# Output projection and memory update in fp16 and column strips, and nine query projections of branch B done in halves in slots 0 to 8

## The chip, the cores and the metric

One core of a Trainium2 chip. The metric is the device time of one execution in microseconds (us). The engines are named as in the profile: PE (TensorE matmul), PEld (TensorE weight load), DVE (VectorE), ACT (ScalarE), POOL (GpSimd), SP (SyncE, which issues most DMAs).

## The reference, cut

```python
# x [1, 2048, 512]; 32 heads of 16; A: 4 segments of 512; B: plain attention
g  = sigmoid((x * gate_w).sum(-1, keepdims=True))
# A: per segment s, M [16 x 16] and z [16] per head carried along
logits = qs @ ks^T * 16**-0.5 + causal_mask(512)
a_dot  = softmax(logits) @ vs
phi    = lambda t: where(t > 0, t + 1, exp(t))
a_mem  = (phi(qs) @ M) / (phi(qs) @ z + 1e-6)
o_s    = sigmoid(beta) * a_mem + (1 - sigmoid(beta)) * a_dot
M += phi(ks)^T @ vs;  z += phi(ks).sum(over positions)
a = concat(o_s) @ A_wo
# B: q, k, v = split(x @ B_wqkv)
b = (softmax(q @ k^T * 16**-0.5) @ v) @ B_wo
return g * a + (1 - g) * b
```

## The kernel before

**Numbers.** Inputs and weights are float32. A projection of x is made from two fp16 parts of each operand: `split` scales a tensor by a power of two and writes `hi` and `lo = raw - hi`. `TERMS = ((0,0),(0,1),(1,0))` are the three products kept, so one projection of a 512-token chunk for 128 channels is 12 matmuls of 512 columns (three terms, four blocks of 128 input channels). The scale comes from the largest magnitude: `peak` reduces on DVE (L379), `top` transposes the statistic on PE (L396) and reduces it, `spread` sends the factors to all partitions by small PE products (L407).

**Phase 1 (0 to 317.87 us).** Sixteen blocks, (group g of 8 heads, segment c) each. A block projects A's q and k (`qk_job`: `qk_mm` on PE, `qk_out` on ACT and DVE, and stores to DRAM by SP), runs A's memory chain, and does as many jobs of the list `fill` as `CUM` says. The memory chain of a block: `mem_out` (phi(q) times M), `mem_put` (transposes, L465, store), `mem_tr` (transposes of phi(k)), `mem_upd` (L488: phi(k) as weights, v with a column of ones as data, 136 columns, float32 in two passes, four 128-token blocks summed; the blocks on the diagonal are picked by a mask and added to M). `fill` holds 16 v projections of B and 24 q and k projections of B (g = 1 to 3); 36 of the 40 are done in the blocks, the last four in slot 0. Between jobs, `spill` puts in products that find the row maxima of the scores of the first units (L565 with the mask products L569; L587).

**Slots.** A unit is four heads against one 512-query chunk, of A (causal) or B (2048 keys). Slot k, of 32, has 37 steps n: 32 of B's unit 32+k and five of A's unit k. Each step (`t_group`) makes two score tiles, keys on partitions (L650, two heads in the two 64-row halves of PE, into a bank of the rotation `T3` = tb0, tb1, mb), then ACT takes the exponential (L656, `raw`), and POOL masks A's diagonal (L659). `pvs(k, n)` multiplies an earlier step's exponentials by v with a column of ones (`pv`, L672: four heads as four strips of 32 output rows in the bank pvb, float32 in two passes). Between the score products the plan puts `s_b` (L587) and DVE's reduction (L589) for the row maxima of the next unit. After n = 20 `m_chain` makes the negative maxima, `m_rows` (L620, n = 24) transposes them. At the end of a unit `fin_copy` (L678) copies pvb, and `fin_load`, `fin_rec`, `fin_bc`, `fin_norm` normalize in later steps.

**The order of the work** is written out: `extras(k)` gives what is done ahead of `pvs` at step n (`pre`) and behind it (`post`), `beside(k, it)` what is done with every second step (it = n // 2). Each engine works through its own list in this order. Four fill jobs stand in slot 0 at n = 0, 2, 4, 6.

**Output projection.** From slot 9 on, row tiles of 128 tokens of finished chunks: `out_split` (ACT copy, POOL subtract) makes `oh`, `ol` in fp32r; `out_mm` makes 12 matmuls for each branch a in two pieces of six (`PIECES`, at n = 1 and 12, `OUT_AT`) into a bank of the rotation (L743), ACT copies the piece (L747, L750) and POOL adds it to `yo` (L751). The two output weights are loaded and split in slots 1 to 4 (`load_wo`, `split_wo`). The last four row tiles are the tail behind slot 31 (`tail_mm`, L773).

Of the kernel before, what the change touches and what calls it, by code (L numbers as in the profile page):

```python
# [42 lines left out]
def gated_mix_kernel(ctx, tc, xt, wq, wk, wv, wo, beta, wqkv, wob, gate_w, out):  # L43
# [298 lines left out]
    def qk_mm(ws, w, c):  # L342
        b = misc()
        n = 0
        for xi, wi in TERMS:
            for k in range(4):
                nc.tensor.matmul(b, WS[ws][w][wi][:, k, :], (XH, XL)[xi][c][:, k, :], start=n == 0, stop=n == 11)  # L347
# [135 lines left out]
    def mem_upd(g, c):  # L483
        pk = PHI.pop((g, "k", c))
        vm = PHI.pop((g, "v", c))
        b = misc()[:, :8 * (E + 1)]
        for i in range(4):
            nc.tensor.matmul(b, pk[:, i, :], vm[:, i].rearrange("p h e -> p (h e)"),  # L488
                             start=i == 0, stop=i == 3)
# [726 lines left out]
```

## Time and profile before

| what | us |
|---|---|
| median of 3 runs (lowest, highest) | 1787.65 (1787.43, 1788.04) |
| the profiled execution | 1788.6 |
| its span in the profile | 1786.9 |
| phase 1 | 0 to 317.87 |
| slot 0 | 64.39 |
| slot 5 | 43.13 |
| slot 15 | 44.85 |
| tail | 1760.07 to 1786.9 |
| mean granted TensorE clock | 0.996 |

In the timeline's rows the columns are start, duration (us), engine, line of the kernel, operation, output<-inputs (partitions x elements and type), and the count of instructions merged into the row; in brackets the idle time ahead of it on its engine and what ended it. A duration of PE includes the pipeline, so that the pace of products is read from the starts of rows. In the rows by group the last numbers are busy time in all, mean ns of one, and the idle time ahead. `<-issue` is a wait that the profile ties to nothing.

### The profile page before, as it was taken

How to read it: one execution, taken by the hardware profiler on the slowest of the kernel's cores; microseconds unless marked ns; L12 is line 12 of the kernel's file. 1: busy time of each engine (PE TensorE's matmuls, PEld its weight loads, DVE VectorE, ACT ScalarE, POOL GpSimd, SP SyncE). 2: the span in 40 equal slices, each digit the busy share in tenths (PEclk: the TensorE clock that was granted, in tenths of full speed). 3: DMA queues.
4: the chain of work that ended last, by engine and by line, in shares of the span. 5: the costliest groups of instructions: out<-in, count | busy, mean ns of one | idle time of the engine just before them, and what ended most of it. 6: DMA issues, size and time to landing. Idle time of an engine off the chain costs nothing.

```text
span 1786.9 us, 43232 instructions
## 1 busy us (share of the span) xinstructions
PE 1756.5 (98%) x17269; PEld 613.8 (34%) x17269; DVE 1559.8 (87%) x1707; ACT 1476.2 (83%) x2797; POOL 363.1 (20%) x739
## 2 busy tenths in 40 slices
PE   8999999899999999999999999999999999999998
PEld 6554445222222222333233333333333333333325
DVE  7745786699999999999999999999999999999932
ACT  4444444599999999999999999999999999999993
POOL 5200000002222111222222222222222222222222
PEclk9999999999999999999999999999999999999999
DMA  5554534332323323232323232323222322323101
GB/s 200 160 151 149 152 108 116 76 80 77 96 80 101 82 64 82 64 94 64 94 64 94 64 93 65 90 68 85 72 79 79 83 75 79 79 78 80 47 29 63
DMA packets 156558, 158.85 MB, mean 89 GB/s; under 512 B 33628, under 2 KB 120636, under 8 KB 156356
## 3 DMA queue, kind: packets, MB, share of 16 engines
q1 hardware_dynamic: 153124, 149.29, 29.9%
q0 software_dynamic: 2944, 6.27, 1.4%
q8 instruction: 136, 2.23, 0.5%
q14 instruction: 66, 0.54, 0.1%
q10 hardware_dynamic: 288, 0.52, 0.1%
HBM read 103.39 MB, written 50.86 MB: 86 GB/s over the span
## 4 chain that ended last, share of the span: by engine, by line
PE 89%; DVE 8%; ACT 1%; DMA 1%; issue 1%; ACTq 0%; SPq 0%; DVEq 0%; POOLq 0%
PE pvb L672 34%; PE tb L650 13%; PE sbk L587 11%; PE mb L650 7%; DVE mxb L589 7%; PE tb L347 3%; PE tb L743 3%; PE sbk L565 2%; PE mb L347 2%; PE pvb L347 2%; PE sbk L317 2%; PE tb L317 2%; PE mb L743 1%; PE sbk L347 1%; PE pvb L317 1%; PE sbk L569 1%
## 5 line engine op out<-in xcount | busy, mean ns | idle before, releaser
L589 DVE TENSOR_REDUCE mxb<-sbk 128x2 f32<-128x1024 f32 x1024 | 1176.6, 1213 | 42.1 <-PE tb L650 19.3
L656 ACT ACTIVATE raw<-tb 128x512 f32<-128x512 f32 x1553 | 880.9, 599 | 49.2 <-PE tb L650 18.2
L672 PE MATMUL pvb<-raw,vb 128*17 128x256 f32 (+1 forms) x7824 | 636.9, 395 | 0.0
L587 PE MATMUL sbk<-kb,qb 64*128 64x512 f16 x2048 | 588.1, 380 | 5.8 <-DVE mxb L589 5.6
L656 ACT ACTIVATE raw<-mb 128x512 f32<-128x512 f32 x783 | 469.1, 599 | 23.7 <-PE mb L650 10.1
L650 PE MATMUL tb<-qb,kb 64*128 64x512 f16 x1339 | 461.7, 381 | 5.0 <-ACT raw L656 3.9
L650 PEld LDWEIGHTS <-kb 64*128 64x128 f16 x2048 | 122.9, 94 | 433.5 <-issue 414.8
L672 PEld LDWEIGHTS pvb<-raw,vb 128*17 128x17 f32 x7824 | 132.4, 95 | 397.0 <-issue 390.9
L650 PE MATMUL mb<-qb,kb 64*128 64x512 f16 x681 | 259.5, 381 | 0.7 <-ACT yp L750 0.7
L659 POOL TENSOR_SCALAR_AFFINE_SELECT raw<-raw 128x256 f32<-128x256 f32 (+1 forms) x320 | 115.3, 361 | 285.8 <-ACT raw L656 277.7
L573 DVE TENSOR_REDUCE mx<-sbk 128x2 f32<-128x1024 f32 (+1 forms) x128 | 133.8, 1087 | 6.7 <-PE sbk L569 5.6
L587 PEld LDWEIGHTS <-qb 64*128 64x128 f16 x2048 | 115.9, 94 | 26.9 <-issue 21.0
L672 PE MATMUL pvb<-raw,va 128*17 128x256 f32 (+2 forms) x1280 | 103.4, 383 | 3.7 <-ACT pvs L678 0.9
L701 POOL TENSOR_TENSOR rec<-rec,grow 128x16 f32<-128x16 f32 x30 | 6.6, 221 | 355.4 <-DVE rec L693 355.4
L713 POOL TENSOR_TENSOR o<-o,d 128x512 f32<-128x512 f32 x31 | 39.5, 1275 | 170.3 <-DMA d<-rd 168.2
L575 DVE TENSOR_REDUCE mx<-sbk 128x4 f32<-128x512 f32 x64 | 60.6, 947 | 12.6 <-PE sbk L569 12.6
L565 PE MATMUL sbk<-ka,qa 64*128 64x512 f16 (+3 forms) x512 | 70.6, 296 | 0.0
L751 POOL TENSOR_TENSOR yo<-yo,yp 128x512 f32<-128x512 f32 x36 | 45.8, 1272 | 80.7 <-ACT yp L750 76.8
L650 PE MATMUL tb<-qa,ka 64*128 64x512 f16 (+3 forms) x340 | 62.0, 302 | 0.0
L362 DVE SCALAR_TENSOR_TENSOR phi<-phe,phi 128x512 f32<-128x512 f32 x24 | 16.6, 692 | 51.2 <-ACT phe L361 51.2
L347 PEld LDWEIGHTS <-ws 128*128 128x128 f16 x384 | 37.9, 100 | 45.4 <-issue 6.1
L569 PE MATMUL sbk<-cmask,crows 64*128 64x64 bf16 x1024 | 52.6, 189 | 0.0
(343 smaller groups left out, 1507.1 us busy)
## 6 DMA issues: line engine op xcount, KB each, us to landing
vb<-vdB SPq DMA_DIRECT2D x16, 1088.0 KB
pd<-pvs SPq DMA_DIRECT2D x64, 256.0 KB
kb<-dB SPq DMA_DIRECT2D x60, 256.0 KB
dB<-st SPq DMA_DIRECT2D x64, 128.0 KB
dA<-st SPq DMA_DIRECT2D x64, 128.0 KB
o<-pd SPq DMA_DIRECT2D x64, 128.0 KB
d<-rd SPq DMA_DIRECT2D x63, 128.0 KB
kb<-dB SPq DMA_DIRECT2D x60, 128.0 KB
```

The costliest lines, as they stand in the source:

```text
L317: nc.tensor.matmul(b, x[:, n % 4, tl * 128:(tl + 1) * 128], (WVA if kd == "A" else WV)[wi][:, n % 4, :], start=n == 0, stop=n == 11)
L347: nc.tensor.matmul(b, WS[ws][w][wi][:, k, :], (XH, XL)[xi][c][:, k, :], start=n == 0, stop=n == 11)
L565: nc.tensor.matmul(b[:, j, c0:c0 + n], q_of(u)[r, p, i * 128:(i + 1) * 128], k_of(u, p)[r, :n], start=True, stop=False)
L569: nc.tensor.matmul(b[:, j, c0 + n - 128 + w.start:c0 + n - 128 + w.stop], crows[r, n2 - 1], cmask[r, n2 - 1, w], start=False, stop=n2 == 2)
L573: nc.vector.tensor_reduce(m[:, :, p, i], b[:, :, :n], axis=AX.X, op=OP.max)
L587: nc.tensor.matmul(b[:, j], q_of(u)[r, p, i * 128:(i + 1) * 128], k_of(u, p)[r, kc * C:(kc + 1) * C], start=True, stop=True)
L589: nc.vector.tensor_reduce(MXB[u][:, :, p, i, kc], b, axis=AX.X, op=OP.max)
L650: nc.tensor.matmul(bs[j][:, c0:c0 + w], k_of(u, h // 2)[r, 128 * it:128 * it + 128], q_of(u)[r, h // 2, q0:], start=True, stop=True)
L656: nc.scalar.activation(pt, bs[j], AF.Exp, scale=AT["esc", kd, qd // 2])
L659: nc.gpsimd.affine_select(out=m, in_=m, pattern=[[1, 128]] if n < 2 else [[0, 2], [1, 128]], compare_op=OP.is_ge, fill=0.0, base=0, channe ...
L672: nc.tensor.matmul(PVB[32 * h:32 * h + E + 1, q0 + lo:q0 + hi], vt[:, it, 4 * q + h, :], pt[:, lo:hi], start=it == 0 and lo == 0, stop=it ...
L743: nc.tensor.matmul(b, (AT["oh"], AT["ol"])[oi][:, g, a], (AT["wh"], AT["wl"])[wi][:, g, a], start=n == 0, stop=n == hi - lo - 1)
```

## The change

Two groups of edits.

*fp16 and strips.* The output weights and the normalized outputs become fp16 pairs: the largest magnitude of the two weights is found in phase 1 (`load_or` loads both in block 0 through POOL's queue into the third and second K buffers, `o_abs` in blocks 2 and 3, `top` in block 4, `o_rng` in block 5), the outputs are scaled by `so` (from the largest magnitudes of v and x; A's v statistic comes from a reduction of `WVA[0]` ahead of block 0), and `back_o` is put into the scale of ACT's copies. `out_mm` writes each product as four strips of 32 output rows; `PIECES` are (0,6), (6,9), (9,12), at n = 1, 12, 20. `mem_upd` makes four strips of 32 rows, each with the two heads that it keeps (34 columns), where all eight heads' columns were made. `m_rows` transposes fp16 operands (`ident16`) and m_chain drops a cast. The weights' load and split go to slots 5 and 6, and 6 and 7 (it = 2 and 12), with one multiply more for each half. The tail uses fp16.

*Halves.* `fill` has 31 jobs, all in the blocks; the nine q projections of B for g = 1 to 3 and c = 1 to 3 (`LATER`) are done one in each of slots 0 to 8. `q_piece` does one half: 12 matmuls of 256 columns into a bank of the rotation, two ACT copies (fp16 `st`, float32 `qraw`), one POOL subtract; behind the second half SP stores both parts. `Q_AT` puts the halves at n = 11 and 19 in slot 0 and n = 1 and 12 in slots 1 to 8. For this x's parts of chunks 1 to 3 and the weights of these jobs (`WQ`) stay in one tile `BIG` beyond phase 1; it later holds the fp16 output weights (`WHL`) and the tail's operands.

```diff
-OUT_AT = (1, 12)
-PIECES = ((0, 6), (6, 12))
+OLOAD = (0, 2, 3, 4, 5)
+Q_AT = ((11, 19), (1, 12))
+OUT_AT = (1, 12, 20)
+PIECES = ((0, 6), (6, 9), (9, 12))
+    def q_piece(g, c, x):
+        h = slice(256 * x, 256 * x + 256)
+        b = misc()[:, :256]
+        for n, (xi, wi, k) in enumerate([(xi, wi, k) for xi, wi in TERMS for k in range(4)]):
+            nc.tensor.matmul(b, WQ[g][wi][:, k, :], (XH, XL)[xi][c][:, k, h], start=n == 0, stop=n == 11)
+        if not x:
+            AT["qs"] = AT["L"].tile([128, 2, C], HF, name="qs")
+        st = AT["qs"]
+        raw = AT["L"].tile([128, 256], FT, name="qraw")
+        nc.scalar.activation(st[:, 0, h], b, AF.Copy, scale=xr[:, c:c + 1])
+        nc.scalar.activation(raw, b, AF.Copy, scale=xr[:, c:c + 1])
+        nc.gpsimd.tensor_tensor(st[:, 1, h], raw, st[:, 0, h], op=OP.subtract)
+        if x:
+            img = QKD["B", 0, g][:, :, c * C:(c + 1) * C]
+            for a in range(2):
+                nc.sync.dma_start(img[:, E * (1 - a):E * (1 - a) + E], st[:, a])
...
 def mem_upd(g, c):
-        b = misc()[:, :8 * (E + 1)]
+        b = misc()[:, :2 * (E + 1)]
         for i in range(4):
-            nc.tensor.matmul(b, pk[:, i, :], vm[:, i].rearrange("p h e -> p (h e)"),
-                             start=i == 0, stop=i == 3)
+            for j in range(4):
+                r = slice(32 * j, 32 * j + 32)
+                nc.tensor.matmul(b[r], pk[:, i, r], vm[:, i, 2 * j:2 * j + 2].rearrange("p h e -> p (h e)"),
+                                 start=i == 0, stop=i == 3)
...
 def m_rows(k):
-            nc.tensor.matmul(b[32 * a:32 * a + 32], m8[:, a], ident, start=True, stop=True)
+            nc.tensor.matmul(b[32 * a:32 * a + 32], m8[:, a], ident16, start=True, stop=True)
...
 def split_wo(g):
+            nc.gpsimd.tensor_scalar(raw, raw, ou, None, op0=OP.mult)
             nc.gpsimd.tensor_copy(AT["wh"][:, g, a], raw)
+    def load_or():
+        for a, w in enumerate((wo, wob)):
+            nc.gpsimd.dma_start(KBF[1 + a], w.rearrange("(k p) c -> p k c", p=128))
+    def o_abs(a):
+        peak(stat(("O", 0), 2)[:, a:a + 1], KBF[1 + a])
+    def o_rng():
+        spread(("O", 0), [(o2[:, 0], o2[:, 1])])
...
 def out_mm(c, t, a, x):
-            nc.tensor.matmul(b, (AT["oh"], AT["ol"])[oi][:, g, a], (AT["wh"], AT["wl"])[wi][:, g, a],
-                             start=n == 0, stop=n == hi - lo - 1)
+            for j in range(4):
+                r = slice(32 * j, 32 * j + 32)
+                nc.tensor.matmul(b[r], (AT["oh"], AT["ol"])[oi][:, g, a, r], (AT["wh"], AT["wl"])[wi][:, g, a],
+                                 start=n == 0, stop=n == hi - lo - 1)
-        nc.scalar.activation(y, b, AF.Copy)
+        nc.scalar.activation(y, b, AF.Copy, scale=back_o)
...
+        if n == 0:
+            peak(stat(("A", 0), 4)[:, 3:4], WVA[0])
...
-    CUM = (2, 4, 6, 9, 11, 13, 16, 18, 20, 22, 24, 27, 29, 32, 34, 36)
+    CUM = (2, 4, 6, 8, 10, 12, 14, 16, 18, 20, 22, 24, 26, 28, 30, 31)
+    LATER = [(g, c) for c in range(1, NC4) for g in range(1, 4)]
...
-        if not k:
-            for n in range(4):
-                pre[2 * n] = [fill[n - 4]]
+        if k < len(LATER):
+            for x, at in enumerate(Q_AT[k > 0]):
+                pre[at] = [todo(q_piece, *LATER[k], x)]
```

How the instructions stand on PE, at three places. First the beginning of slot 0. In the program before (L650 score products, tb and mb banks; L587 row-maximum products, sbk banks; L347 a projection of B's fill list, xp and xq the two parts of x):

```order
L465 MATMUL tb_139<-ident,om 128x128 x4
L650 LDWEIGHTS kb_89
L650 MATMUL tb_138<-qb_70,kb_89 128x512
L587 LDWEIGHTS qb_68
L587 MATMUL sbk_142<-kb_90,qb_68 128x512
...
L650 MATMUL mb<-qb_70,kb_89 128x512
L347 LDWEIGHTS wv_105
L347 MATMUL tb_139<-xp_99,wv_105 128x512
...
L347 MATMUL tb_139<-xq_103,wv_105 128x512
```

The changed program at the same place (L514 is L465 of before, L699 L650, L639 L587, L721 L672):

```order
L514 MATMUL pvb<-ident,om 128x128 x4
L699 LDWEIGHTS kb_90
L699 MATMUL tb_134<-qb_70,kb_90 128x512
L639 LDWEIGHTS qb_68
L639 MATMUL sbk_138<-kb_91,qb_68 128x512
...
L699 MATMUL tb_135<-qb_70,kb_90 128x512
L699 LDWEIGHTS kb_90
L699 MATMUL mb<-qb_70,kb_90 128x512
```

The projection behind the first step is gone; the next step's score product follows directly.

Second, the place in slot 0 where the changed program has the first half (n = 11; L409, its operands in the tile big):

```order
L699 MATMUL mb<-qb_70,kb_90 128x512
L409 LDWEIGHTS big
L409 MATMUL tb_134<-big 128x256
...
L721 MATMUL pvb<-raw_87,vb_75 17x256 x4
L699 LDWEIGHTS kb_90
L699 MATMUL tb_135<-qb_70,kb_90 128x512
```

Twelve such products stand between the step's second score product and its four PV strips; the bank tb_134 is taken by them, so the next step has tb_135.

Third, the second piece of the output projection in slot 9. Before, at n = 12 (L743, wl and wh the weights' parts, oh and ol the outputs'):

```order
L650 MATMUL tb_138<-qb_70,kb_89 128x512
L743 MATMUL mb<-wl,oh 128x512 x2
L743 MATMUL mb<-wh,ol 128x512 x4
L650 LDWEIGHTS kb_89
L650 MATMUL tb_139<-qb_70,kb_89 128x512
```

In the changed program the last piece, at n = 20 (L808, a strip of 32 rows in each row):

```order
L699 MATMUL tb_135<-qb_70,kb_90 128x512
L808 LDWEIGHTS ol
L808 MATMUL mb<-big,ol 32x512
...
L721 MATMUL pvb<-raw_87,vb_75 17x256 x4
L699 LDWEIGHTS kb_90
L699 MATMUL tb_134<-qb_70,kb_90 128x512
```

Six products at n = 12 have become three sets of four strips there and three more at n = 20, where nothing but the step's own products stood; each set takes its four loads.

More of the change, by code (lines that the diff above doesn't have):

```diff
@@ L151, in identity @@
         nc.vector.tensor_scalar(ident, jp, 0.0, None, op0=OP.is_equal)
+        nc.gpsimd.tensor_copy(ident16, ident)
         for j in range(2):
@@ L254, in do_beta @@
         nc.vector.tensor_scalar(nq, nq, -1.0, 1.0, op0=OP.mult, op1=OP.add)
+        for t in (gh, nh):
+            nc.vector.tensor_scalar(t, t, so[:, 1:2], None, op0=OP.mult)
     def do_gate():
@@ L294, in split_wv @@
     def split_wv(k):
-        split(WV[0][:, k, :], WV[1][:, k, :], WR["B", "v", k], vu)
+        split(WV[0][:, k, :], WV[1][:, k, :], WR["B", "v", k], vu[:, 0:1])
     def load_w_raw(kd, g, w, eng=None):
@@ L304, in load_w, with w_home @@
         WR[kd, g] = [load_w_raw(kd, g, w) for w in range(2)]
+    def w_home(n, kd, g, w):
+        return WQ[g] if kd == "B" and g and not w else WS[n][w]
     def split_w(n, kd, g, ws=(0, 1)):
         for w in ws:
-            split(WS[n][w][0], WS[n][w][1], WR[kd, g][w], wu[:, "AB".index(kd), g, w:w + 1])
+            split(*w_home(n, kd, g, w), WR[kd, g][w], wu[:, "AB".index(kd), g, w:w + 1])
     TERMS = ((0, 0), (0, 1), (1, 0))
@@ L346, in qk_mm @@
             for k in range(4):
-                nc.tensor.matmul(b, WS[ws][w][wi][:, k, :], (XH, XL)[xi][c][:, k, :], start=n == 0, stop=n == 11)
+                nc.tensor.matmul(b, ws[wi][:, k, :], (XH, XL)[xi][c][:, k, :], start=n == 0, stop=n == 11)
                 n += 1
@@ L901, in gated_mix_kernel @@
     fill = [todo(v_job, "B", tt) for tt in range(NT)]
-    fill += [todo(qk_job, 2 - g % 2, "B", g, w, c) for g, c2 in ((1, 0), (1, 2), (2, 0), (3, 0), (2, 2), (3, 2))
-             for c in (c2, c2 + 1) for w in range(2)]
+    fill += [todo(qk_job, 2 - g % 2, "B", g, w, c)
+             for g, cs in ((1, (0, 1, 2, 3)), (2, (0, 1)), (3, (0, 1)), (2, (2, 3)), (3, (2, 3)))
+             for c in cs for w in range(c > 0, 2)]
+    LATER = [(g, c) for c in range(1, NC4) for g in range(1, 4)]
     nf = 0
@@ L960, in gated_mix_kernel @@
                 f()
+        if blk == OLOAD[0]:
+            load_or()
+        if blk in OLOAD[1:3]:
+            o_abs(OLOAD.index(blk) - 1)
+        if blk == OLOAD[3]:
+            top(("O", 0))
+        if blk == OLOAD[4]:
+            o_rng()
         if blk == 14:
@@ L986, in gated_mix_kernel @@
                 load_kb(1, 1 + n)
-            if nf == 35:
+            if nf == len(fill) - 1:
                 mode["misc"] = [MB, PVB, TB[1]]
@@ L991, in gated_mix_kernel @@
                 spill()
[L992 to L997 removed]
+                if nf in (14, 17):
+                    load_w("B", 2 + nf // 17)
+                if nf in (15, 18, 22):
+                    split_w(2 if nf == 18 else 1, "B", (15, 18, 22).index(nf) + 1)
+                for f, at in ((w_abs, (11, 15, 19)), (lambda *a: top(a), (12, 16, 20)), (w_rng, (13, 17, 21)),
+                              (w_esc, (14, 18, 22))):
                     if nf in at:
@@ L1156, in gated_mix_kernel @@
                     load_vb(k // 2 + 1)
-                if 1 <= k <= 4:
-                    load_wo(k - 1)
-            if it == 12 and 1 <= k <= 4:
-                split_wo(k - 1)
+                if k in (5, 6):
+                    load_wo(2 * k - 10)
+                    load_wo(2 * k - 9)
+            if it in (2, 12) and k in (6, 7):
+                split_wo(2 * k - 12 + it // 12)
     pv(31, 2)
```

98 lines of the change are left out of this document (58 added, 40 removed).

## The prediction

> **What bounds the kernel now.** I read the page first, then the span cut into stages, then single stretches of TensorE's timeline, since each part of the change lies in another stage. The profiled execution took 1788.6 us, 0.95 over the median of the runs; the sum below is made against it.
>
> ```profile
> PE 89%; DVE 8%; ACT 1%; DMA 1%; issue 1%; ACTq 0%; SPq 0%; DVEq 0%; POOLq 0%
> ```
>
> TensorE (PE) carries 89% of the chain that ends last, VectorE (DVE) 8%. The stages are not alike. The windows below are slot 0, slot 5 and slot 15; after the length come busy time and count of PE, weight loads, DVE, ACT and POOL, then granted clock, DMA share and GB/s.
>
> ```profile
> 317.87:382.26 64.39, 58.80 (x529) 17.44 (x529) 52.83 (x54) 44.53 (x82) 3.27 (x10) 0.95 0.27 78
> 555.38:598.51 43.13, 42.53 (x486) 12.06 (x486) 42.71 (x42) 40.52 (x77) 5.30 (x18) 1.00 0.24 66
> 997.30:1042.15 44.85, 44.76 (x497) 13.57 (x498) 43.00 (x42) 42.09 (x80) 8.95 (x20) 1.00 0.24 62
> ```
>
> Slots 1 to 8 (43.13 in slot 5) are DVE's: 42.71 busy. Slots 9 to 30 (44.85 in slot 15) are PE's: 44.76 busy, 0.11 idle. Slot 0 is neither's wholly (58.80 and 52.83 of 64.39), with the lowest clock. Before slot 0, 317.87 us of projections are PE's.
>
> **Phase 1: five projections fewer.** The fill list falls by nine jobs: four from slot 0, five from the blocks.
>
> ```profile
> 186.04 1.90 PE L347 MATMUL tb<-xp,ws 128*128 128x512 f16 x8
> 187.78 1.03 PE L347 MATMUL tb<-xq,ws 128*128 128x512 f16 x4
> 188.64 0.63 PE L449 MATMUL tb<-mst,phi 128*128 128x136 f32 x4
> ...
> 195.39 0.60 PE L465 MATMUL tb<-ident,om 128*128 128x128 f32 x4
> 195.83 0.38 PE L347 MATMUL mb<-xp,ws 128*128 128x512 f16 x1
> ...
> 271.11 0.22 PE L569 MATMUL sbk<-cmask,crows 64*128 64x64 bf16 x4
> 271.17 0.22 PE L565 MATMUL sbk<-ka,qa 64*128 64x128 f16 x2
> ...
> 271.60 1.19 PE L488 MATMUL mb<-vm,pk 128*128 128x136 f32 x8
> 272.63 0.59 PE L347 MATMUL pvb<-xp,ws 128*128 128x512 f16 x2
> ```
>
> A job is 12 matmuls in 188.64 - 186.04 = 2.60 us, 216 ns each. PE is full here, so 5 x 2.59 = -12.95.
>
> *Memory strips.* mem_upd is now 8 records in 1.03 (271.60 to 272.63), 129 ns each; at other places 0.93, so I count 116 a record. It becomes eight sets of four strips of 34 columns, with two switches of array form. No row shows such a set. Below: the mask products, 64 columns with their own loads, start 4 in 0.06, so a set may cost 28 ns (34/64 of that); above: a set costs what a 128-column float32 pass does, (195.83 - 195.39)/4 = 110 ns. With 0.19 for the switches (below) that is 0.41 to 1.07 against 0.93. I take 54 ns, four starts of 13.5, since the mask row is nearest in width: 0.62, so -0.31 x 12 = -3.7 (ends -6.2 and +1.7). The Trainium skill, "TensorEngine Tiling (Array Packing)", section Instruction Overhead, says that every matmul carries about 60 cycles and that a dimension that is already small should not be split; by that an estimate of 25 ns for each of the 384 strip passes makes 9.6 and the switches 2.3, against 11.2 now: +0.7, and the whole sum 4.4 higher. The mask row, at 13.5 a matmul, speaks against that; no run yet shows strips so narrow.
>
> *Statistics of the output weights.* Two top() and spread chains for O: two pairs of small PE products, 0.31 each: +0.6. DVE gets three reductions of 2048 columns.
>
> ```profile
> L379 DVE TENSOR_REDUCE stat<-kb 128x1 f32<-128x2048 f32 x2 | 4.5, 2280 | 0.0
> ...
> 63.95 1.28 DVE L280 SCALAR_TENSOR_TENSOR xq<-kb,xu,xp 128x1024 f16<-128x1024 f32 x1 [0.28 <-ACT xp L279]
> ...
> 69.49 0.16 DVE L879 TENSOR_REDUCE stat<-stat 128x1 f32<-128x4 f32 x1
> ...
> 69.86 0.38 PE L396 MATMUL tb<-ident,stat 128*3 128x128 f32 x2
> ```
>
> The one ahead of block 0 stands in front of the statistic that PE waits for at 69.86; DVE ends it at 69.65, 0.2 before PE takes it, and has idled 0.28 not long before, so 2.28 - 0.2 - 0.28 = +1.8. The two in blocks 2 and 3 delay DVE's share of a job by 2.28, which PE's three jobs of lead mostly take: +1.0 for both and for a weight statistic that now stands one job after its load (0 to +4). The two 1 MB loads go out on POOL's queue in block 0, behind nothing PE needs then; 0 (cover gone: the K images of block 2 come late).
>
> Phase 1: -12.95 - 3.7 + 0.6 + 1.8 + 1.0 = **-13.25**.
>
> **Slot 0: four projections gone, two halves in.**
>
> ```profile
> 318.98 1.23 DVE mxb L589
> ...
> 322.62 0.10 ACT raw L656
> ...
> 327.26 4.60 PE mb L347 x12
> ```
>
> The chain shows ACT reading its eight scale registers until 322.62, then four jobs; this one takes 4.60 for the 12 matmuls that took 2.60 in phase 1: TensorE's clock is down after that wait (0.95 over the slot). Removed with them are DVE's four copies of st, some 0.75 each, 3.0. What is left for DVE is 52.83 - 3.0 = 49.8 and its 0.4 idle of other slots, the floor. To that come the wait at the start, 2.4 (DVE done with its first tasks at 320.2, exps from 322.6), and 1 for a clock that may still halve after it: 53.4, so **-11.0**. Ends: 50.2 (-14), or only two jobs at 2.60 and the 2.0 of one slow one gained (-7). The halves stand at n = 11 and 19, late enough to fall under DVE's floor: PE has 58.80 - 14.4 (two jobs at 4.60, two at 2.60) + 3.0 = 47.4.
>
> **Slots 1 to 8: two halves each.** A half is 12 matmuls of 256 columns into the next score bank. Half of 216 is 108, measured 110 for the 128-column float32 pass of as many cycles: 12 x 0.110 = 1.32, plus 0.18 for the PV switches on both sides: 1.5, so 3.0 a slot. Part fills stalls that are there. In slot 2:
>
> ```profile
> 427.75 0.38 PE L650 MATMUL tb<-qb,kb 64*128 64x512 f16 x1
> ...
> 428.63 0.37 PE L650 MATMUL tb<-qb,kb 64*128 64x512 f16 x1 [0.29 <-ACT raw L656]
> ...
> 429.66 0.39 PE L650 MATMUL mb<-qb,kb 64*128 64x512 f16 x1
> ...
> 439.74 0.68 PE L650 MATMUL tb<-qb,kb 64*128 64x512 f16 x2
> 440.63 0.39 PE L587 MATMUL sbk<-kb,qb 64*128 64x512 f16 x2 [0.22 <-DVE mxb L589]
> ...
> L750 ACT ACTIVATE yp<-tb 128x512 f32<-128x512 f32 x23 | 13.7, 597 | 14.1 <-PE tb L743 14.0
> ```
>
> From 427.75 to 429.66 one group takes 1.91 instead of 1.09: it waits for a bank that ACT empties. This 0.82 at n = 2, one of 0.5 at n = 13 (440.63, behind DVE's bank; two products of 0.22 started at 439.74), and some 0.3 of small ones are PE time that the halves at n = 1 and 12 use: 3.0 - 1.6 = +1.4, less 0.1 of m_rows: **+1.3 x 8 = +10.4**. Ends: DVE's 42.7 against PE's 42.53 + 3.0 = 45.5: +0.6 (all slack used) and +2.4. Each half adds two ACT copies (0.35 estimated from 597 ns for 512 columns), 1.4 a slot on 40.5 of 43.1; they precede the next exp, whose bank they hold one group longer; that is in the upper end. POOL's subtract, then SP's two stores stand ahead of SP's fin_bc; SP is not waited for within a slot, 0.
>
> **Slots 9 to 30: the output product in fp16 strips.**
>
> ```profile
> 729.22 0.39 PE L650 MATMUL tb<-qb,kb 64*128 64x512 f16 x1
> ...
> 729.75 1.20 PE L743 MATMUL tb<-wh,oh 128*128 128x512 f32 x4
> 730.79 0.62 PE L743 MATMUL tb<-wl,oh 128*128 128x512 f32 x2
> 731.34 0.39 PE L650 MATMUL tb<-qb,kb 64*128 64x512 f16 x1
> ...
> 731.57 0.38 PE L650 MATMUL mb<-qb,kb 64*128 64x512 f16 x1
> 731.87 0.63 PE L672 MATMUL pvb<-raw,vb 128*17 128x256 f32 x8
> 732.43 0.39 PE L650 MATMUL tb<-qb,kb 64*128 64x512 f16 x1
> ...
> 731.87 0.13 PEld L672 LDWEIGHTS pvb<-raw,vb 128*17 128x17 f32 x8 [0.42 <-issue]
> ...
> L672 PEld LDWEIGHTS pvb<-raw,vb 128*17 128x17 f32 x7824 | 132.4, 95 | 397.0 <-issue 390.9 <-PE sbk L587 0.9 <-ACT raw L656 0.4
> ...
> L347 PEld LDWEIGHTS <-wv 128*128 128x128 f16 x288 | 27.6, 99 | 36.8 <-issue 8.7
> ...
> 626.87 0.39 PE L620 MATMUL tb<-ident,m 128*32 128x128 f32 x4
> 627.20 0.39 PE L650 MATMUL mb<-qb,kb 64*128 64x512 f16 x1
> ```
>
> A piece of six float32r products is 731.34 - 729.75 = 1.59: 232 each and one first at 337. A strip set is priced by PV, the same form: 732.43 - 731.87 = 0.56 for two sets of 512 column cycles with one switch of 0.10 in it (a score product before PV takes 0.30, another 0.22-0.23), so 0.23 a set. Six sets are 1.38. At n = 1 they stand directly against PV, which has the same form, so the switch and the slow first product go: -0.13. The second piece is halved, at n = 12 and 20, three sets 0.69 each instead of one 1.5: n = 12 then no longer stalls, n = 20 gains work; -0.73 + 0.69 = -0.04. m_rows goes from four float32 records, 0.33, to two: -0.105. Together -0.275 x 22 = **-6.05** (ends: 0 and -0.5 x 22; a stall left between the exps takes back the first, a cleaner n = 12 gives the second). Slot 15 would be near 44.6. ACT's third copy (0.60) goes on 42.09 of 44.85 (94%): PE's group of 1.09 covers it, though a third copy at n = 20 stands between exps; POOL's third add of 1.27 goes on 8.95 busy.
>
> The weight split moves from slots 1 to 4 (at n = 25) to slots 6 and 7 (n = 5 and 25), with a multiply more for each half.
>
> ```profile
> 412.78 1.27 POOL L729 TENSOR_TENSOR wl<-o,wh 128x512 fp32r<-128x512 f32 x1
> 420.35 0.29 POOL L659 TENSOR_SCALAR_AFFINE_SELECT raw<-raw 128x128 f32<-128x128 f32 x1 [6.30 <-ACT raw L656]
> ```
>
> In slot 1 it ends at 414.05, 6.3 ahead of POOL's masks; two multiplies, at most 1.27 each, leave 3.8 free: 0.
>
> **Slot 31 and tail.** Slot 31 gets three pieces for each branch at n = 28 with one copy buffer, so two more copies of 0.60 are waited for: +1.2, less 0.3 as in other slots; the tail's 96 float32r products, priced 232 as in a piece, go to 216: 96 x 0.016 = -1.5, none of it hidden, as PE is the last to end there before the copies: **-0.6.**
>
> **Sum.** -13.25 - 11.0 + 10.4 - 6.05 - 0.6 = -20.5: 1788.6 - 20.5 = 1768.1 profiled, 1767 as a median.
>
> **Rivals.**
> 1. *More is hidden* (0.17): halves cost only the DVE floor, +0.6 a slot (-5.6), and slot 0 falls to 49 or 50 (-4): 1757. For it: DVE's 42.71 of 43.13; against it: ACT's stalls come with each extra bank taken.
> 2. *Slot 0 saves little* (0.17): the start wait and the halved clock stay and, without the jobs, PE is idle there; -4 instead of -11, and the statistics cost 3 more: 1777. For it: the 0.95 clock and the 4.60.
> 3. *Loads show* (0.06): each of a half's 256-column products waits for its own load of 99 (12 x 18 x 0.099 = +21): 1788, no change. Against it: 128-column products every 110 with a load each (195.39).
> 4. *Slower: strips load one after the other* (0.05). If the four loads of a set are not overlapped, 4 x 95 = 380 against 229, and 12 sets for each branch, 2 branches, 12 row tiles are 288 sets x 0.151 = +43.5: 1810. It decides from +71 ns a set (20.5/288). Against it: PV's eight loads take 0.13 together. The same page of the Trainium skill, section Gotcha 2, says that column tiling excludes the fast weight load; the sum with this is rival 4's.
>
> **Numbers.** My forecast (1761 to 1773) has 0.55, the rivals 0.17, 0.17, 0.06 and 0.05. 1750 to 1783 reaches rivals 1 and 2 with their ends and leaves 3 and 4 out. A measurement of this kernel tells about 0.2%, 3.6 us. Faster by more: 0.90 (all of the forecast, rivals 1 and 2, a little of 3); within: 0.04; slower: 0.06 (rival 4 and the rest of 3).
>
> **What would show it.** Right: phase 1 ends near 304.5; slot 0 takes 53 to 54 with DVE busy over 0.9 of it; slots 2 to 8 take 44.4, the 0.82 stall at n = 2 gone; slots 9 to 29 44.6; strip sets 0.23 apart. Wrong: a half over 1.6, slot 0 over 58, DVE waiting for PE in slots 1 to 8, or a strip set over 0.30.

## The result and the profile after

The changed kernel took 1773.47 us in the median of four runs (1770.93 to 1776.16), the kernel before 1787.85: ratio 0.9921, 95% interval 0.9909 to 0.9933, so 14 us faster. Forecast were 1767 and a gain of 20.5; the time lies half a microsecond above the 1761 to 1773 that had the chance of 0.55, and inside 1750 to 1783. The profiled execution of the change took 1775.42 us, its span is 1773.7. The chain of waits of its page begins:

```profile
PE 91%; DVE 4%; ACT 2%; DMA 1%; issue 1%; POOL 0%; SPq 0%; ACTq 0%; DVEq 0%; POOLq 0%
```

TensorE has a still larger share, DVE half of its former one: the slots that DVE bounded (1 to 8) are now TensorE's. The windows of slots 0, 5 and 15, of slot 31 (to 0.07 behind the first tail product at 1747.26), and of the tail, columns as in the prediction:

```profile
308.61:363.22 54.61, 49.50 (x504) 14.77 (x504) 50.19 (x49) 43.53 (x82) 4.62 (x12) 0.97 0.26 72
542.08:586.82 44.74, 44.65 (x508) 13.66 (x508) 43.07 (x42) 41.81 (x81) 6.51 (x19) 1.00 0.34 94
987.66:1032.11 44.45, 44.36 (x531) 12.28 (x532) 42.89 (x42) 42.56 (x81) 9.84 (x20) 1.00 0.26 67
1698.41:1747.33 48.92, 44.22 (x372) 10.49 (x372) 10.90 (x23) 42.37 (x84) 14.82 (x21) 0.97 0.10 32
1747.33:1773.70 26.37, 20.82 (x96) 9.21 (x96) 10.20 (x26) 3.37 (x9) 5.02 (x9) 0.96 0.24 79
```

Slot 31 of the kernel before, beside which the fourth of these rows is read:

```profile
1714.69:1760.07 45.38, 43.26 (x302) 12.36 (x301) 11.22 (x24) 40.88 (x82) 12.52 (x19) 1.00 0.10 34
```

| stage | before | after | measured | forecast |
|---|---|---|---|---|
| phase 1 | 317.87 | 308.61 | -9.3 | -13.25 |
| slot 0 | 64.39 | 54.60 | -9.8 | -11.0 |
| slots 1 to 8 | 345.64 | 357.71 | +12.1 | +10.4 |
| slots 9 to 30 | 986.79 | 977.48 | -9.3 | -6.05 |
| slot 31 and tail | 72.2 | 75.3 | +3.1 | -0.6 |
| sum of the spans | 1786.9 | 1773.7 | -13.2 | -20.5 |

### The profile page after: what moved, and what is told of

Its sections match the earlier page's. It is cut to its first block, busy times and chain, and to the rows that moved or that the text cites. A ratio compares the mean times of both kernels' runs of the same rounds, so it can differ in the third digit from the quotient of the medians.

```text
span 1773.7 us, 45701 instructions
## 1 busy us (share of the span) xinstructions
PE 1734.9 (98%) x18467; PEld 571.0 (32%) x18467; DVE 1562.7 (88%) x1713; ACT 1496.0 (84%) x2848; POOL 410.7 (23%) x762
## 4 chain that ended last, share of the span: by engine, by line
PE 91%; DVE 4%; ACT 2%; DMA 1%; issue 1%; POOL 0%; SPq 0%; ACTq 0%; DVEq 0%; POOLq 0%
PE pvb L721 36%; PE tb L699 15%; PE sbk L639 12%; PE mb L699 7%; PE tb L376 3%; PE tb L808 3%; PE sbk L617 2%; PE mb L376 2%; DVE mxb L641 2%; ACT raw L705 1%; PE pvb L345 1%; PE sbk L345 1%; PE pvb L376 1%; PE mb L808 1%; PE tb L345 1%
## 5 line engine op out<-in xcount | busy, mean ns | idle before, releaser
L721 PE MATMUL pvb<-raw,vb 128*17 128x256 f32 (+1 forms) x7824 | 637.1, 396 | 0.0
L639 PE MATMUL sbk<-kb,qb 64*128 64x512 f16 x2048 | 597.1, 381 | 4.5 <-DVE mxb L641 4.4
L705 ACT ACTIVATE raw<-mb 128x512 f32<-128x512 f32 x762 | 456.6, 599 | 23.3 <-PE mb L699 6.8
L699 PE MATMUL tb<-qb,kb 64*128 64x512 f16 x1377 | 471.4, 382 | 3.9 <-ACT raw L705 2.1
L699 PEld LDWEIGHTS <-kb 64*128 64x128 f16 x2048 | 118.5, 94 | 445.7 <-issue 430.0
L721 PEld LDWEIGHTS pvb<-raw,vb 128*17 128x17 f32 x7824 | 134.3, 95 | 396.0 <-issue 386.8
L699 PE MATMUL mb<-qb,kb 64*128 64x512 f16 x642 | 244.7, 381 | 2.1 <-ACT yp L815 1.7
L816 POOL TENSOR_TENSOR yo<-yo,yp 128x512 f32<-128x512 f32 x60 | 76.3, 1272 | 189.3 <-ACT yp L815 189.3
L639 PEld LDWEIGHTS <-qb 64*128 64x128 f16 x2048 | 110.9, 94 | 16.3 <-issue 15.5
L721 PE MATMUL pvb<-raw,va 128*17 128x256 f32 (+2 forms) x1280 | 103.3, 383 | 3.7 <-ACT pvs L727 0.9
L617 PE MATMUL sbk<-ka,qa 64*128 64x512 f16 (+3 forms) x512 | 70.9, 296 | 1.9 <-DVE mx L625 1.9
L627 DVE TENSOR_REDUCE mx<-sbk 128x4 f32<-128x512 f32 x64 | 60.6, 947 | 13.2 <-PE sbk L621 13.2
L699 PE MATMUL tb<-qa,ka 64*128 64x384 f16 (+3 forms) x322 | 61.8, 297 | 0.0
L621 PEld LDWEIGHTS <-crows 64*128 64x128 bf16 x1024 | 46.5, 94 | 15.0
```

What stands on the lines that cost most here:

```text
L617: nc.tensor.matmul(b[:, j, c0:c0 + n], q_of(u)[r, p, i * 128:(i + 1) * 128], k_of(u, p)[r, :n], start=True, stop=False)
L621: nc.tensor.matmul(b[:, j, c0 + n - 128 + w.start:c0 + n - 128 + w.stop], crows[r, n2 - 1], cmask[r, n2 - 1, w], start=False, stop=n2 == 2)
L639: nc.tensor.matmul(b[:, j], q_of(u)[r, p, i * 128:(i + 1) * 128], k_of(u, p)[r, kc * C:(kc + 1) * C], start=True, stop=True)
L699: nc.tensor.matmul(bs[j][:, c0:c0 + w], k_of(u, h // 2)[r, 128 * it:128 * it + 128], q_of(u)[r, h // 2, q0:], start=True, stop=True)
L705: nc.scalar.activation(pt, bs[j], AF.Exp, scale=AT["esc", kd, qd // 2])
L721: nc.tensor.matmul(PVB[32 * h:32 * h + E + 1, q0 + lo:q0 + hi], vt[:, it, 4 * q + h, :], pt[:, lo:hi], start=it == 0 and lo == 0, stop=it ...
```

## The experiments

All kernels are edits of the changed kernel. The table has the stage lengths of each one's profiled execution in us; "idle" is TensorE's idle time in phase 1 (the gaps between the end of a product and the start of the next), "clock" what phase 1 lost to a granted clock below 1.00 (the sum of 2 x (1 - clock) over windows of 2 us). The last column is the median of the runs.

| kernel | phase 1 | idle | clock | slot 0 | slots 2-8 | slots 9-29 | slot 31 | median |
|---|---|---|---|---|---|---|---|---|
| before | 317.87 | 5.0 | 3.4 | 64.39 | 43.13 | 44.88 | 45.38 | 1787.85 |
| changed | 308.61 | 14.0 | 3.4 | 54.60 | 44.71 | 44.45 | 48.84 | 1773.47 |
| changed, again | 310.92 | 12.1 | 6.8 | 54.60 | 44.71 | 44.45 | 48.76 | 1773.79 |
| memory update wide | 308.05 | 10.0 | 0 | 55.30 | 44.71 | 44.46 | 48.42 | 1774.39 |
| no halves | 314.06 | 10.2 | 0 | 64.50 | 43.14 | 44.45 | 48.68 | 1779.74 |
| output products whole | 308.90 | 12.1 | 5.1 | 55.35 | 44.71 | 44.54 | 48.86 | 1776.50 |
| two output pieces | 308.08 | 12.1 | 3.4 | 54.64 | 44.71 | 44.58 | 45.45 | 1774.87 |
| slot 31 multiply on DVE | 305.00 | 12.1 | 1.7 | 54.52 | 44.71 | 44.45 | 47.06 | 1774.17 |
| v peak early | 309.46 | 12.7 | 5.1 | 55.01 | 44.71 | 44.45 | 48.65 | 1774.22 |
| no output statistics | 309.08 | 12.0 | 6.8 | 54.97 | 44.71 | 44.47 | 48.88 | 1773.18 |
| registers early | 308.53 | 12.6 | 3.4 | 53.68 | 44.71 | 44.45 | 48.48 | 1773.06 |
| one projection piece | 305.08 | 12.1 | 1.7 | 55.52 | 45.71 | 44.45 | 48.84 | 1783.88 |
| three edits for slots 0 and 31 | 308.52 | 12.4 | 3.4 | 53.63 | 44.70 | 44.45 | 44.11 | 1767.77 |

Slots 2 to 30 agree to hundredths between executions; phase 1 does not. The changed kernel, its repetition, and the three kernels that alter only slots 9 to 31 (whole products, two pieces, DVE) run the same phase 1 code, and so does the one with one piece: 305.00 to 310.92. Without the clock's loss it is 303.3 to 305.2, mean 304.1. So a difference in phase 1 is read below as the length without clock loss (the length minus the column "clock"), and only above 2 us. Each kernel has one profile, while its median is of 4 to 10 runs. Where the profiled run was the shortest of its kernel (1769.41 for the multiply on DVE, 1779.70 for one piece), the lengths add up to less than the median.

**The changed kernel again**

> The changed kernel itself again, on the chip of the two kernels beside it. Its four runs went from 1770.9 to 1776.2. Theory (TensorE's clock is halved for 3.4 us at a time behind idle stretches, once to four times in phase 1 and slots 0 and 31; each costs 1.7 us, and the stages between do not move): median 1772 to 1775, slots 2 to 30 within 0.05 us of the first profile, phase 1 between 304.5 and 309. Rival (the spread comes from the long middle of the program): slots 2 to 30 differ by over 2 us in sum.

The slots stood still and phase 1 moved, somewhat beyond the 304.5 to 309 expected, with 6.8 us of clock loss. In most places the clock falls for about 3.4 us (a loss of 1.7), in some for twice as long without a break (80 to 88 of this profile). The same windows of the change's first profile, and of the kernel with slot 31's multiplication moved, whose phase 1 has the same instructions:

```profile
74.00:78.00 4.00, 2.19 (x11) 1.19 (x12) 2.48 (x9) 1.22 (x2) 0.00 (x0) 1.00 0.49 163
...
82.00:86.00 4.00, 4.00 (x14) 1.78 (x14) 2.95 (x6) 0.62 (x2) 0.00 (x0) 0.58 0.50 133
```

```profile
74.00:78.00 4.00, 4.00 (x26) 2.66 (x27) 3.01 (x17) 2.51 (x4) 0.00 (x0) 1.00 0.54 191
...
82.00:86.00 4.00, 4.00 (x20) 1.84 (x19) 3.08 (x13) 1.40 (x4) 0.00 (x0) 1.00 0.72 188
```

Where TensorE was busy 2.19 us of 4, the clock of 82 to 86 is 0.58; where it was busy throughout, it stays at 1.00. The idle time came from a store: ACT had no free st buffer until one had landed, TensorE's statistic stood behind that on DVE. ACT's and TensorE's rows of the first profile:

```profile
73.85 0.69 ACT L392 ACTIVATE st<-sbk,xr 128x512 f16<-128x512 f32 x1 [4.18 <-DMA dB<-st]
75.81 0.38 PE L453 MATMUL tb<-wdiag,ones 4*128 4x4 f32 x2 [1.82 <-DVE wdiag L446]
```

In the other profile there is no such gap at TensorE, but both have one of 1.14 to 1.15 near 70. The pair does not show that the gap brought the fall. The kernel before has no gap at this place and falls for longer:

```profile
70.00:78.00 8.00, 8.00 (x49) 4.88 (x47) 5.57 (x21) 4.20 (x7) 0.00 (x0) 1.00 0.30 92
78.00:86.00 8.00, 8.00 (x29) 4.22 (x29) 3.49 (x7) 2.33 (x5) 0.00 (x0) 0.57 0.38 104
```

And of the five other profiles of this phase 1, all with the gap near 70 and none with the one at 74, three show a fall near 80 (the control, whole products, two pieces) and two do not (DVE, one piece). Another candidate stands ahead of the place in every profile: 32 products of a single column, 75.78 to 80.01 in the kernel before, 78.19 to 82.03 with two pieces, and 76.77 to 80.25 in the second of the profiles above, whose clock does not fall. TensorE counts as busy in them. So neither the gap nor these products alone decide whether the clock falls. Near 300 and in slot 0 idle stretches of up to 2.8 us stand ahead of the falls. The cause stays open, as no run changed either by itself. The Trainium skill, "TensorE: Matmul & The Clock Gate", section Part 1: The HAM clock gate, describes a gate that halves the clock behind idle windows of about 3.4 us and releases it after as long a busy one; the length of the slow stretch agrees in most places here (0.58 over 4 us), while no idle window of 3.4 us stands ahead of a fall near 80.

**Memory update wide**

```diff
...
-            for j in range(4):
-                r = slice(32 * j, 32 * j + 32)
-                nc.tensor.matmul(b[r], pk[:, i, r], vm[:, i, 2 * j:2 * j + 2]..., start=i == 0, stop=i == 3)
+            nc.tensor.matmul(b, pk[:, i, :], vm[:, i]..., start=i == 0, stop=i == 3)
...
```

> The changed kernel with mem_upd as before: 136 columns, four float32 products for each of its twelve calls. Theory (the strips' gain of 13.33 - 7.81 = 5.5 us of TensorE time is on the path): phase 1 ends at 314 instead of 308.6, the time is 5 to 6 us above the changed kernel's. Rival (TensorE waits 14 us in phase 1 of the changed kernel, so that what the strips save is given back in waits): phase 1 ends at 309 to 311.5, the time is 0 to 3 us above.

The rival fits the total: 1774.39 against 1773.47 and 1773.79, and phase 1 at 308.05 against 305.0 to 310.9. The strips themselves are shorter than hoped. An update with nothing to wait for, in strips and in the wide form, with the projections around it:

```profile
96.84 0.59 PE L376 MATMUL mb<-big,ws 128*128 128x512 f16 x2
97.36 0.46 PE L539 MATMUL sbk<-vm,pk 128*32 128x34 f32 x32
97.75 0.82 PE L376 MATMUL sbk<-big,ws 128*128 128x512 f16 x3
```

```profile
92.68 1.24 PE L376 MATMUL mb<-big,ws 128*128 128x512 f16 x5
93.76 1.09 PE L537 MATMUL sbk<-vm,pk 128*128 128x136 f32 x8
94.69 0.59 PE L376 MATMUL sbk<-big,ws 128*128 128x512 f16 x2
```

From its start to the next product an update takes 0.39 in strips (12.3 ns for each of 32 passes, with the switch behind them) and 0.93 in the wide form; ahead of the strips a switch to the other array form adds 0.09 (two projection products in 0.52, where they take 0.43 otherwise). So 0.44 is saved here, and up to 0.64 where a score or mask product stands ahead and the wide form takes a switch too (1.03). The 13.33 and 7.81 in the expectation are from start to start with the waits in them, 1.2 and 2.8 us. One of these waits, behind the last update:

```profile
291.56 0.46 PE L539 MATMUL mb<-vm,pk 128*32 128x34 f32 x32
293.35 0.39 PE L639 MATMUL sbk<-kb,qb 64*128 64x512 f16 x2 [1.33 <-DVE mxb L641]
```

TensorE waits 1.33 for DVE's reduction there. What became of the saving: TensorE's busy time in phase 1 is 291.35 in the wide form, and 288.00 in the first profile of the change, of which 3.4 are clock loss, so 6.8 us less work; its idle time is 14.0 there and 12.1 in most profiles instead of 10.0. Without clock loss, the wide form is 308.05 against 304.1: the strips are worth about 4 us where the clock holds, and about 1 in the medians. The clock takes most of the difference: the wide form's four runs all have a mean granted clock of 0.998, the nine of the changed kernel 0.994 to 0.997, 0.9957 in the mean. As an estimate, a loss of 0.002 and of 0.0043 of 1772 us is 3.5 and 7.7 us. Why the strips' runs lose more to the clock is not shown.

**No halves**

```diff
...
-    CUM = (2, 4, 6, 8, 10, 12, 14, 16, 18, 20, 22, 24, 26, 28, 30, 31)
+    CUM = (2, 4, 6, 9, 11, 13, 16, 18, 20, 22, 24, 27, 29, 32, 34, 36)
...
-        if k < len(LATER):
-            for x, at in enumerate(Q_AT[k > 0]):
-                pre[at] = [todo(q_piece, *LATER[k], x)]
+        if not k:
+            for n in range(4):
+                pre[2 * n] = [fill[n - 4]]
```

The order of the fill list, and what hangs on its numbers, go back with it.

> The changed kernel with the fill list of before: 36 jobs in the blocks, four in slot 0, no halves in slots 0 to 8; fp16, strips and statistics stay. Theory (the five jobs taken out of phase 1 had covered waits there: TensorE's idle time grew from 5.0 to 14.0 us and falls back to 7 to 9): phase 1 ends near 315.5, slot 0 takes 64, slots 2 to 8 take 43.0, in all 1778 to 1780. Rival (the added statistics make the waits, whatever the number of jobs): idle stays at 14, phase 1 ends at 321 to 322, in all 1784 to 1786.

The first theory holds: 314.06, 64.50, 43.14 a slot, 1779.74. Idle time falls less than thought (10.2). Without clock loss, five jobs are worth 314.1 - 304.1 = 10.0 us, not 12.95. Of the other 3, about 2 are waits that the jobs had covered (idle 12.1 in most profiles against 10.2); the rest is within what phase 1 resolves. The moved projections are worth 6 us in all (1779.74 to 1773.5), and the fp16 and strip edits the other 8 (1787.85 to 1779.74).

**Output products whole**

```diff
-            for j in range(4):
-                r = slice(32 * j, 32 * j + 32)
-                nc.tensor.matmul(b[r], (...)[oi][:, g, a, r], ...)
+            nc.tensor.matmul(b, (...)[oi][:, g, a], ...)
```

> The changed kernel with the output products in fp16 as whole 128-row products, pieces and places unchanged. Theory A (what gained in slots 9 to 30 is fp16 and the three pieces; a strip set takes as long as a whole product, and strips save one switch of form only where PV follows at n = 20): 44.5 to 44.6 instead of 44.44 a slot, 1 to 3 us in all. Theory B (as predicted, strips save the switch and the slow first product in each piece): 44.75 a slot, +7 us. Theory C (strips cost: 236 ns for a set against 216 for a product): 44.2, -5 us.

Theory A: 44.54 a slot, +0.1. In the change a set of strips is no faster than a whole product. Slot 9, pieces at n = 1, 12 and 20:

```profile
722.78 1.48 PE L808 MATMUL tb<-big,oh 128*32 128x512 f16 x24
724.19 0.39 PE L699 MATMUL mb<-qb,kb 64*128 64x512 f16 x1
...
735.73 0.61 PE L808 MATMUL tb<-big,oh 128*32 128x512 f16 x8
736.17 0.39 PE L808 MATMUL tb<-big,ol 128*32 128x512 f16 x4
736.49 0.39 PE L699 MATMUL tb<-qb,kb 64*128 64x512 f16 x1
...
745.14 0.83 PE L808 MATMUL mb<-big,ol 128*32 128x512 f16 x12
745.80 0.60 PE L721 MATMUL pvb<-raw,vb 128*17 128x256 f32 x8
```

Six sets take 1.41, 0.235 each with a switch at the end; three take 0.76 where score products follow and 0.66 where PV, of the same form, does. With whole products, six take 1.40 and three 0.75 in either place. That 0.1 at n = 20 is all that the strips add.

**Two output pieces**

```diff
-OUT_AT = (1, 12, 20)
-PIECES = ((0, 6), (6, 9), (9, 12))
+OUT_AT = (1, 12)
+PIECES = ((0, 6), (6, 12))
```

> The changed kernel with two output pieces of six at n = 1 and 12, in strips. Theory (the gain of slots 9 to 30 beyond my sum comes from the third piece, which lets n = 12 pass without starving ACT): slots 9 to 30 take 44.7, like the slots 1 to 8 of the changed kernel with two pieces of 1.42 at the same places, +5.7 us in all; slot 31 has one copy less for each branch and comes back by 1 to 2.5, so that the sum is +3 to +5. Rival (my sum: three pieces are worth 0.04): 44.45 to 44.5, and with slot 31 the time is 0 to 2 us lower.

Between the two: 44.58, so the third piece is worth 0.13 a slot (2.9 us over 22), more than my 0.04 and half of the theory's 0.26. What both missed is slot 31: 45.45 instead of 48.84, so the third piece costs 3.4 us there and the kernel with two pieces is no slower (1774.87).

**Slot 31's multiplication on DVE**

```diff
-            nc.gpsimd.tensor_tensor(o, o, AT["d"][0][:64], op=OP.mult)
+            nc.vector.tensor_tensor(o, o, AT["d"][0][:64], op=OP.mult)
```

> The changed kernel with one multiplication of slot 31 (o by d at it = 13, which waits for a DMA) on DVE instead of POOL. Theory (it heads POOL's queue until the DMA lands at 1731.2, the add of yo stands behind it, so that ACT's next copy into the one buffer yp waits 2.84 and 1.37 us and with it the exponentials): slot 31 is 2.5 to 4 us shorter than the 48.9 us of the changed kernel. Rival (the three copies into one buffer cost it by themselves): 0 to 1 us shorter.

Neither: 47.06, 1.8 shorter in the profile; the median of the runs, 1774.17, does not show it. ACT's copies and POOL in the changed kernel:

```profile
1731.21 1.27 POOL L1173 TENSOR_TENSOR o<-o,d 64x512 f32<-64x512 f32 x1 [7.51 <-DMA d<-rd]
1732.44 1.26 POOL L816 TENSOR_TENSOR yo<-yo,yp 128x512 f32<-128x512 f32 x1
```

```profile
1730.20 0.69 ACT L815 ACTIVATE yp<-tb,backo 128x512 f32<-128x512 f32 x1
1733.73 0.69 ACT L815 ACTIVATE yp<-tb,backo 128x512 f32<-128x512 f32 x1 [2.84 <-POOL yo L816]
1735.79 0.69 ACT L815 ACTIVATE yp<-mb,backo 128x512 f32<-128x512 f32 x1 [1.37 <-POOL yo L816]
```

and ACT's with the multiplication on DVE:

```profile
1729.19 0.69 ACT L815 ACTIVATE yp<-tb,backo 128x512 f32<-128x512 f32 x1 [1.92 <-POOL yo L816]
1731.25 0.69 ACT L815 ACTIVATE yp<-mb,backo 128x512 f32<-128x512 f32 x1 [1.37 <-POOL yo L816]
```

The queue behind the DMA made 0.9 of the wait at the second copy and the late start of the first add; the rest, 1.92 and 1.37, is the one buffer: copy 0.69, add 1.27, each three times in turn, as one branch's three pieces all stand at n = 28. ACT, which had no wait above 0.2 us in this slot until then, stands meanwhile.

**V peak early**

```diff
     constants()
+    peak(stat(("A", 0), 4)[:, 3:4], WVA[0])
...
-        if n == 0:
-            peak(stat(("A", 0), 4)[:, 3:4], WVA[0])
```

> The changed kernel with the peak of A's v weights (2.28 us on DVE) taken near 12 us instead of ahead of the second k projection at 60 us. Theory (that reduction delays the statistic for which TensorE waits at 70.9 and 75.8, and what it costs is TensorE's 1.14 + 1.82 us): phase 1 is 2 to 3 us shorter. Rival (DVE is late there anyway, or the waits move to the next dependence): less than 1 us shorter.

The rival: 309.46, and 304.4 without clock loss, against 304.1. The wait at 70.9 (1.14) is gone, that at 75 (1.58 in this profile) is not.

**No output statistics** (the loads, reductions, transpositions and spread of the output weights' scale left out, constants in their place):

> The changed kernel without the statistics of the output weights: no loads in block 0, no reductions in blocks 2 and 3, no transposition and spread in blocks 4 and 5; the two scales are constants. Theory A (my sum: they cost 0.6 on TensorE and about 1 in DVE's delays): phase 1 is 1 to 2 us shorter. Theory B (they make the new waits): 4 to 6 us shorter. Theory C (waits of fewer jobs remain and swallow it): 0 to 0.7.

302.3 without clock loss, 1.8 below the mean, 0.3 to 0.6 in the medians: theory A or C, which the 2 us that phase 1 resolves cannot tell apart; theory B is out.

**Registers early**

```diff
+        if blk == 14:
+            for ri, rk in enumerate("AB"):
+                for rg in range(4):
+                    AT["esc", rk, rg] = nc.scalar.alloc_register(...); nc.scalar.reg_load(...)
...
```

The loop that read them behind phase 1 is taken out.

> The changed kernel with ACT's eight scale registers read at block 14 instead of after phase 1. Theory (the wait of the first exponentials for these reads is on the path at the start of slot 0, 2.4 us in my sum): phase 1 and slot 0 together 2 to 3.5 us shorter, and less of the halved clock behind it. Rival (DVE's reductions bound slot 0, so that a start of ACT that is earlier only waits later): less than 1 us.

The rival: 53.68, 0.9 less. The chain of waits at the start of slot 0, in the change and with registers early:

```profile
309.80 2.27 DVE mxb L641 x2
312.08 0.64 ACTq L1182
312.71 0.08 issue
312.80 1.09 ACT raw L705 x2
```

```profile
309.72 3.41 DVE mxb L641 x3
313.12 0.04 issue
313.17 0.39 PE sbk L639 x2
```

ACT's reads leave the chain, and DVE's third reduction is there instead.

**One projection piece**

```diff
-Q_AT = ((11, 19), (1, 12))
+Q_AT = ((11,), (1,))
-        h = slice(256 * x, 256 * x + 256)
+        h = slice(0, C)
...
```

> The changed kernel with each late query projection in one piece of 12 products of 512 columns, at n = 11 in slot 0 and n = 1 in slots 1 to 8, two copies of 512 columns. Theory A (the slots are bound by TensorE's work alone, 44.71 with two halves of 1.42): 2.6 + 0.1 instead of 2.83, so 44.5 to 44.6 for slots 2 to 8. Theory B (halving matters: one gap of 2.7 us between score products empties the banks that ACT reads, and the stall of 0.57 at n = 13 that the second half had filled is back): 45.0 to 45.4.

Theory B, and more: 45.71 a slot, ratio 0.998 to the kernel before (0.9971 to 0.999). The projection itself is shorter, 2.70 instead of 2.83, but ACT has nothing to read for 1.58 us, and TensorE then waits for its bank:

```profile
545.97 2.76 PE L409 MATMUL tb<-big 128*128 128x512 f16 x12
...
550.09 0.37 PE L699 MATMUL tb<-qb,kb 64*128 64x512 f16 x1 [0.26 <-ACT qraw L415]
```

```profile
548.77 0.69 ACT L414 ACTIVATE qs<-tb,xr 128x512 f16<-128x512 f32 x1 [1.58 <-PE tb L409]
549.36 0.68 ACT L415 ACTIVATE qraw<-tb,xr 128x512 f32<-128x512 f32 x1
```

The next two groups of score products take 1.42 and 1.35 us instead of 1.09 and 1.25, and the stall at n = 13 is back.

**Three edits for slots 0 and 31** (registers early, the multiplication on DVE, and in slot 31 the output product in one piece for each branch):

```diff
...
+        one = ((0, 12),)
-        for n, ats in [(k - 9, OUT_AT)] + [(23, (2 * OMI,) * len(PIECES))] * (k == 31):
+        for n, ats, ps in ([(k - 9, OUT_AT, PIECES)] if k < 31 else [(22, (12,), one), (23, (2 * OMI,), one)]):
...
```

> The changed kernel with three edits: ACT's scale registers read at block 14; slot 31's multiplication on DVE; in slot 31 the last row tile's output product in one piece of twelve for each branch, at n = 12 and 28, so one ACT copy for each branch instead of three. Theory A (slot 31 is bound by ACT, 41.2 of 46.6 busy, and by POOL's queue): slot 31 takes 44.5 to 45.5 instead of 48.8, slot 0 53.7 instead of 54.6, in all 4 to 5.5 us below the changed kernel: 1768 to 1769.5. Theory B (one piece leaves ACT without banks for 2.8 us): slot 31 takes 46.5 to 47.5, in all 2 to 3 below.

Theory A, a little better: slot 31 takes 44.11, slot 0 53.63, and the time is 1767.77 us (1765.40 to 1768.53; ratio to the kernel before 0.9887, 0.9872 to 0.9902), 6.0 below the changed kernel beside it (1773.79). It beats both kernels. Its windows of slot 0 and slot 31:

```profile
308.52:362.15 53.63, 49.41 (x503) 14.70 (x504) 50.12 (x49) 43.51 (x82) 4.60 (x12) 0.97 0.27 74
1697.28:1741.38 44.10, 42.14 (x371) 10.71 (x371) 11.58 (x24) 39.86 (x80) 8.73 (x16) 1.00 0.11 36
```

ACT has 39.86 to do instead of 42.37, and the clock of slot 31 is 1.00 instead of 0.97. Each of the two pieces still leaves ACT waiting for 1.40, less than the 4.2 for POOL's adds of the changed kernel:

```profile
1712.86 0.69 ACT L812 ACTIVATE yo<-tb,backo 128x512 f32<-128x512 f32 x1 [1.40 <-PE tb L808]
1730.71 0.69 ACT L815 ACTIVATE yp<-tb,backo 128x512 f32<-128x512 f32 x1 [1.40 <-PE tb L808]
```

## Why the prediction was right, point by point

The direction and the order of size were right, and so was the sign of each stage but that of slot 31 and tail; the gain was a third smaller than the sum. The stages came out against their forecasts by +4.0 (phase 1), +1.2 (slot 0), +1.7 (slots 1 to 8), +3.7 (slot 31 and tail) and -3.3 (slots 9 to 30). That the last one offsets part of the others is luck. In the medians the clock has a part too: the mean granted clock is 0.9976 over the thirty runs of the kernel before that stand beside the experiments and 0.9957 over the nine of the changed kernel, by estimate 4.3 and 7.7 us. Rival 1 (0.6 a slot for the halves, slot 0 at 49 or 50) did not come, nor did rival 2 (slot 0 only 4 us shorter). By the steps of the sum:

- *Jobs in phase 1* (-12.95): mis-sized. Five jobs are worth 10.0 without clock loss. TensorE was taken as full, and the jobs' cover of its waits for DVE and for stores was priced at nothing. TensorE's idle time went from 5.0 to 14.0; without halves it is 10.2, so the jobs are a part of that and not all.
- *Memory strips* (-3.7, TensorE's time 0.62 an update against 0.93): mis-sized. An update takes 0.39 and 0.09 for the switch ahead, against 0.93, so that TensorE's work falls by more than forecast, 6.8 us in phase 1. But waits, then the clock, take it back: about 4 us are left where the clock holds, about 1 in the medians. The prediction's estimate of 25 ns for a pass, worked out from the Trainium skill, "TensorEngine Tiling (Array Packing)", section Instruction Overhead, is twice the measured 12.3 ns, switch included. The measurement decides, and the +0.7 that followed from it did not come.
- *V peak* (+1.8): moving it saved nothing that phase 1 resolves. *Statistics* (+1.6): 1.8 without clock loss and 0.3 to 0.6 in the medians, not resolved either.
- *Slot 0* (-11.0): -9.8. DVE is the floor as said: 50.19 busy of 54.61. The wait for registers was charged 2.4 and is worth 0.9. The terms of the forecast (49.8, 0.4, 2.4 and 1) add up to 53.6, not 53.4.
- *Halves* (+1.3 a slot): +1.6 in slots 2 to 8, +1.0 in slot 1. A half takes 1.42, not 1.50:

```profile
543.94 1.49 PE L409 MATMUL mb<-big 128*128 128x256 f16 x12
545.35 0.39 PE L699 MATMUL tb<-qb,kb 64*128 64x512 f16 x1
```

  The stalls of 0.82 and 0.5 are filled as said; the "0.3 of small ones" are not there, and TensorE's 44.65 busy of 44.74 is the new bound. DVE waiting for PE, named as a sign of being wrong, came (1.3 us in slot 5, 0.2 before); the forecast itself, 44.4 a slot with DVE at 42.7, implied it. Rival 3 (loads that show) is out: 118 ns a product, first and last included.
- *Output strips* (-0.275 a slot): -0.43. m_rows saved 0.16 instead of 0.105 (0.32 to 0.16), n = 1 gave -0.18 for -0.13, and the third piece is worth 0.13 instead of 0.04; the prediction's own figures (one piece of 1.5 against two of 0.69) make 0.12. These parts overlap, as they add up to 0.47. The reason given was wrong in part: the strips are 0.1 of the 0.43, and with whole fp16 products it is 0.33 (44.54). fp16 was not changed by itself. Rival 4 is out at 0.235 a set.
- *Slot 31* (+0.9): the step that failed. It counted two more copies of 0.60 and not that a copy waits for POOL's add of 1.27 through one buffer when the pieces follow one another, with ACT as the bound, nor that POOL's queue was held by a DMA: +3.5. It also put both branches' pieces at n = 28; one branch has them at 1, 12 and 20. With two pieces slot 31 takes 45.45, about what it takes in the kernel before (45.38), so the third piece is the 3.4.
- *Tail* (-1.5): TensorE's products took 20.8 instead of 22.6, -1.8. The end behind the last product was 5.5 instead of 4.1 us here and 3.9 to 5.5 in the experiments with the same tail, 4.35 in the changed kernel again, so the change does not set it. The last copy ends at 1769.25, and what follows to 1773.70 is the landing of the stores.

## What to carry to other kernels

Work that is taken off an engine at its limit is worth its full time only until the next wait that it had covered: count the waits that stand beside it first. An added copy into a single buffer that follows another at once costs its whole round (copy, reader, and what the reader's queue waits for) where the copying engine is the bound; with the pieces spread over a slot the third copy came with a gain. Split a filler so that it is shorter than what the next engine has ahead of it: two pieces of 1.42 cost 1.6 us a slot, one of 2.70 cost 2.6.

## What was not expected of the hardware

The granted clock halved for about 3.4 us, or twice that, at one to three places in phase 1, a loss of 1.7 to 6.8 us in executions of identical code; this, and not the long middle part, spreads the changed kernel's runs over 5 us. The kernel before shows such a fall (0.57 over 8 us) behind 8 us in which TensorE was busy throughout; what sets it off is not shown. Strips of 34 columns with their own loads passed at 12.3 ns a pass, the switch behind them included, where eight wide passes of 136 columns took 116 ns each. Six sets of four strips of 512 columns took 1.41 us and six whole products 1.40.
